# Local attention units taken in pairs on four 64x64 tiles, PSUM as one tile, and a new order of the work

## The chip, the cores and the metric

The kernel runs on one core of a Trainium2 chip. The metric is the time of one execution on the device in microseconds (us), lower is better. Inputs are prepared on the host before the launch (laid out, padded, sliced), and this is not timed.

## The reference

Eight sequences (B = 8) of S = 576 tokens with 8 heads of 64 go through two kinds of attention, whose sum is mixed by a Fourier transform and then sent through a feed-forward layer:

```
q_d, k_d, v_d = means over groups of 4 tokens           # 144 of 576 positions
out_up    = repeat(softmax(q_d k_d^T / 8) v_d, 4)
out_local = softmax(where(|i - j| < 4, q k^T / 8, -1e9)) v
x  = out_up + out_local                                 # [8, 576, 512]
u  = x + real(fft(fft(x, axis=1), axis=2))
un = (u - mean) / sqrt(var + 1e-6)
out = u + max(un @ w1, 0) @ w2                          # w1 512x2048, w2 2048x512, given in float64
```

## The kernel before

The work falls into two stages. The first handles attention and the Fourier mix, sequence by sequence. The second is the feed-forward layer over 36 tiles of 128 tokens, in nine blocks of four tiles.

**Local units.** The band |i - j| < 4 is covered by windows of 64 tokens that start 57 apart. A `Unit` (line 525) holds two windows of one sequence, all 8 heads, so there are 5 units a sequence and 40 in all. The two windows lie on the two halves of the partitions: rows 0-63 and rows 64-127. For each unit `scores` puts the mask into one PSUM bank with two matmuls (line 559) and adds 16 matmuls of 64x64 (line 566), heads times halves. The tile that lies on rows 0-63 writes partitions 0-63, the other writes 64-127. `maxima` (line 579) is one VectorE reduction, `exps` scales the maxima and takes one ScalarE exponential per head (line 584), `transpose_p` turns the probabilities with four matmuls into another bank, `copy_p` brings them back to SBUF, `values` multiplies by v with 16 matmuls into two banks (line 625; column 65 gives the row sum), and `result` divides: two small additions (line 639), one reciprocal, and two products (line 643; four products of half the rows for the middle unit of a sequence). A matmul of 32-bit floats (not a transpose) stands in the trace as two, so a burst of one unit's scores or values shows as 32 matmuls.

**Pooled attention.** `Pooled` (line 416) does two heads at a time on 72 partitions: scores into two banks, two maxima (line 443), four exponentials, eight transposes into two banks, two copies (line 475), values (line 483) and a division. Each of its two heads has a bank, and an instruction never spans two.

**Fourier mix.** `Mix` (line 675) folds the sequence into sums and differences on VectorE and GpSimd, splits each 32-bit operand into a high and a low part, multiplies by sine and cosine matrices (lines 744 and 789), and stores to DRAM. `sequence` gives four outputs of 290 columns, each evacuated by one ScalarE copy (line 751) and one VectorE subtraction (line 754). `store_local` writes the local attention's result of a sequence to DRAM in ten transfers at one place in the order.

**Feed-forward layer.** For each of 16 slices f of the hidden layer `Block.first` has 12 matmuls of 128x512 (line 958), `high` and `low` evacuate (lines 962, 966), `second` has 12 more (lines 976 to 978). Blocks 0 and 1 take f = 0 to 4 first, then f = 5 to 15, and then come the other seven blocks. Each weight quarter (`Quarter`, four per f) is fetched by SyncE and decoded from float64 by ScalarE, GpSimd (line 342), VectorE (lines 350, 353, 356), ScalarE and GpSimd (line 371). `CHUNKS` says which f have their place in SBUF from the start (f < 3); the others get places when earlier pools are closed, the next ones at `close_a`, which frees the local units' tiles.

**PSUM.** Eight banks. `bank()` (line 395) hands them out in turn, from two pools; at `close_a` four of them go to the accumulators of the feed-forward layer and four stay in turn.

**Order.** Every step is an event, and the events are issued in the order of the numbers in `TURNS` (a name's numbers go to its calls one after the other), so each engine's queue and each DMA queue is in program order as that table has it. An instruction that waits holds back all that stand behind it on its engine. Loads and stores stand in SyncE's queue, the accumulating loads (`vsum` and the feed-forward layer's `ut`) in GpSimd's.

Of the kernel before, what the change touches and what calls it, by code (L numbers as in the profile page):

```python
# [17 lines left out]
NUM_V, NUM_QKT, NUM_P = 3, 6, 2  # L18
NUM_PT = 2

KEPT = 290
# [6 lines left out]
        3, 7, 11, 26, 46, 82, 84, 101, 156, 213, 246, 262, 231, 263, 351, 378, 401, 448, 494, 526, 562, 586,  # L28
        622, 665, 729, 748, 826, 898, 883, 900, 993, 1048,
    ),  # L30
    "Pooled.scores": (
        18, 19, 35, 39, 81, 110, 124, 175, 222, 224, 283, 321, 382, 383, 466, 468, 547, 569, 598, 628, 706, 722,
        786, 809, 873, 906, 905, 927, 1014, 1036, 1060, 1130,
    ),
    "Pooled.maxima": (
        21, 23, 48, 66, 89, 117, 137, 188, 228, 244, 300, 327, 390, 413, 482, 512, 574, 578, 609, 641, 715, 736,
        804, 839, 878, 911, 928, 960, 1021, 1044, 1076, 1134,
    ),
    "Pooled.exps": (
        25, 30, 50, 71, 95, 128, 161, 194, 236, 275, 308, 332, 395, 427, 492, 518, 582, 596, 619, 648, 726, 764,  # L40
        813, 843, 885, 920, 954, 987, 1028, 1055, 1090, 1136,
    ),
    "Pooled.transpose_p": (
        28, 37, 56, 80, 107, 144, 173, 199, 252, 286, 328, 345, 418, 435, 497, 531, 588, 600, 627, 672, 740,
        783, 829, 848, 907, 924, 972, 994, 1034, 1067, 1131, 1139,
    ),
    "Pooled.copy_p": (
        32, 53, 69, 86, 127, 160, 177, 209, 277, 307, 331, 366, 426, 461, 502, 534, 595, 617, 645, 685, 761,
        790, 832, 850, 919, 955, 989, 998, 1053, 1093, 1135, 1145,
    ),  # L50
    "Pooled.values": (
        41, 55, 77, 91, 143, 174, 181, 214, 285, 319, 340, 380, 430, 464, 521, 544, 599, 624, 668, 703, 782,
        808, 845, 858, 925, 969, 995, 1003, 1069, 1114, 1138, 1147,
    ),
    "Pooled.result": (
        63, 64, 88, 97, 165, 187, 189, 226, 318, 326, 372, 388, 446, 486, 536, 554, 634, 635, 678, 710, 805,
        825, 866, 867, 959, 975, 1007, 1019, 1108, 1133, 1155, 1158,
    ),
    "Pooled.store": (105, 291, 403, 565, 728, 942, 1096, 1188),
    "Pooled.pack": (103, 233, 399, 561, 727, 882, 1031, 1164),  # L60
    "Mix.half_sum": (
        118, 112, 133, 266, 270, 268, 408, 438, 442, 577, 630, 638, 730, 737, 769, 895, 931, 910, 1059, 1043,
        1079, 1166, 1205, 1191,
    ),
    "Mix.half_difference": (
        121, 99, 142, 260, 248, 302, 421, 449, 452, 585, 613, 614, 744, 750, 774, 912, 913, 914, 1049, 1050,
        1083, 1172, 1177, 1196,
    ),
    "Mix.channels": (
# [4 lines left out]
    ),  # L74
    "Mix.fold": (
# [4 lines left out]
    ),  # L80
    "Mix.split_high": (
# [79 lines left out]
    ),  # L161
    "constants": (83,),
    "clear_yz": (93,),
    "close_b": (1193,),
    "close_a": (1226,),
    "close_e": (1304,),
    "close_d": (1401,),
# [1034 lines left out]
```

## Time and profile before

| | |
|---|---|
| median of 3 runs | 1155.38 us (1148.1 to 1157.35) |
| the profiled execution | 1145.82 us, span 1144.0 us |
| busy: TensorE / VectorE / ScalarE / GpSimd | 1108.0 / 545.4 / 358.4 / 293.5 us |
| mean granted clock of TensorE | 0.99 |
| moved by DMA | 123.07 MB |

Names in the profile: PE is TensorE, PEld its weight loads, DVE VectorE, ACT ScalarE, POOL GpSimd, SP SyncE. A busy time is counted once where instructions overlap. "L566" is line 566 of the kernel. In a timeline or chain "x32" means 32 instructions taken together. The chain is the sequence of instructions and waits that ended last, followed back from the end.

### The profile page before, as it was taken

The numbers are of one execution on the slowest core, as the hardware profiler recorded it, in microseconds if no ns is written. First come the engines' busy times: TensorE is split into PE (matmuls) and PEld (weight loads), VectorE is DVE, ScalarE is ACT, GpSimd is POOL, SyncE is SP. The second block draws the span as 40 slices with busy tenths as digits, with TensorE's granted clock in tenths as the row PEclk, the third lists the DMA queues.
The fourth block names the chain that finished last, engine by engine and source line by source line (L and its number), as shares of the span: only waits on it lengthen the run. The fifth ranks groups of instructions, "written<-read, shape, count | busy, mean of one in ns | idle before, by whom it ended". The sixth has DMA issues, their size and how long they took to land.

```text
span 1144.0 us, 20389 instructions
## 1 busy us (share of the span) xinstructions
PE 1108.0 (97%) x8172; PEld 935.8 (82%) x8172; DVE 545.4 (48%) x1226; ACT 358.4 (31%) x1050; POOL 293.5 (26%) x411
## 2 busy tenths in 40 slices
PE   7899999899889999999999999999999999999998
PEld 6788888889778788888888888888888888888886
DVE  4889999899878776322212222222222222222111
ACT  4777767767544443111111111111111111111110
POOL 2444545355574553203002002001101100200000
PEclk7999999999999999999999999999999999999999
DMA  8888777777685332506006005105103302400000
GB/s 257 269 257 252 215 240 247 234 217 181 181 188 161 109 123 93 110 1 148 1 1 147 1 1 129 19 1 121 27 1 95 53 1 71 77 1 37 1 1 37
DMA packets 57901, 123.07 MB, mean 108 GB/s; under 512 B 7280, under 2 KB 7408, under 8 KB 57552
## 3 DMA queue, kind: packets, MB, share of 16 engines
q1 hardware_dynamic: 44288, 92.23, 24.6%
q0 software_dynamic: 13520, 29.55, 14.7%
q8 instruction: 64, 1.05, 0.4%
q14 instruction: 29, 0.24, 0.1%
HBM read 89.88 MB, written 30.74 MB: 105 GB/s over the span
## 4 chain that ended last, share of the span: by engine, by line
PE 79%; DVE 10%; DMA 6%; issue 2%; SPq 1%; ACT 1%; POOL 0%; DVEq 0%; ACTq 0%; POOLq 0%
PE hps L958 34%; PE acc L976 11%; PE acc L978 11%; PE acc L977 11%; DMA vsum<-in_vg_dram 3%; PE y L744 2%; PE av L625 1%; PE avd L483 1%; PE sc L566 1%; PE tpn L932 1%; DVE sums L552 1%; DMA raw<-in_wq_dram 1%; PE mix L789 1%; DVE xeo L710 1%; DVE w L697 1%
## 5 line engine op out<-in xcount | busy, mean ns | idle before, releaser
L966 DVE SCALAR_TENSOR_TENSOR hl<-hps,hh 128x512 fp32r<-128x512 f32 x144 | 99.1, 690 | 456.3 <-ACT hh L962 456.3
L958 PE MATMUL hps<-unT,w1h 128*128 128x512 f32 x1152 | 309.9, 392 | 0.0
L962 ACT ACTIVATE hh<-hps 128x512 fp32r<-128x512 f32 x144 | 86.0, 598 | 539.2 <-PE hps L958 533.9
L958 PEld LDWEIGHTS hps<-unT,w1h 128*128 128x128 f32 x1152 | 215.5, 188 | 45.7
L976 PE MATMUL acc<-w2h,hh 128*128 128x512 f32 x576 | 227.3, 395 | 0.2 <-ACT hh L962 0.2
L978 PE MATMUL acc<-w2h,hl 128*128 128x512 f32 x576 | 225.5, 392 | 0.0
L977 PE MATMUL acc<-w2l,hh 128*128 128x512 f32 x576 | 225.4, 391 | 0.0
L958 PE MATMUL hps<-unT,w1l 128*128 128x512 f32 x576 | 155.2, 392 | 0.0
L978 PEld LDWEIGHTS acc<-w2h,hl 128*128 128x128 f32 x576 | 108.3, 188 | 24.0 <-DVE hl L966 0.4
L958 PEld LDWEIGHTS hps<-unT,w1l 128*128 128x128 f32 x576 | 108.3, 188 | 23.6
L976 PEld LDWEIGHTS acc<-w2h,hh 128*128 128x128 f32 x576 | 108.3, 188 | 23.4 <-ACT hh L962 0.6
L977 PEld LDWEIGHTS acc<-w2l,hh 128*128 128x128 f32 x576 | 108.3, 188 | 22.4
L917 POOL TENSOR_TENSOR rstd<-rstd,mhalf 128x1 f32<-128x1 f32 x36 | 19.9, 554 | 300.3 <-DVE rstd L916 299.1
L902 POOL DMA_DIRECT2D ut<-ux x40 | 35.5, 1002 | 206.7 <-DMA ut<-um 206.3
L584 ACT ACTIVATE sb<-sc,mx 128x64 f32<-128x64 f32 x320 | 69.8, 329 | 2.0 <-PE tpl L596 0.8
L941 DVE TENSOR_TENSOR unT<-tpn,unT 128x512 fp32r<-128x512 f32 x36 | 24.8, 688 | 55.4 <-ACT unT L938 55.4
L552 DVE TENSOR_REDUCE sums<-qkT 128x224 f32<-128x896 f32 (+4 forms) x48 | 44.4, 945 | 11.0 <-DMA qkT<-in_qk_dram 9.2
L566 PEld LDWEIGHTS sc<-qkT 64*64 64x64 f32 x1280 | 46.1, 141 | 3.8 <-DMA qkT<-in_qk_dram 0.6
L625 PE MATMUL av<-vaug,pT 64*64 64x65 f32 x1280 | 47.4, 224 | 1.3 <-DMA vaug<-in_vw_dram 0.7
L724 POOL TENSOR_TENSOR fl<-xeo,fh 128x512 fp32r<-128x512 f32 x32 | 42.0, 1334 | 21.8 <-ACT fh L721 16.3
L625 PEld LDWEIGHTS av<-vaug,pT 64*64 64x64 f32 x1280 | 42.2, 138 | 6.3 <-issue 2.9
L566 PE MATMUL sc<-qkT 64*64 64x64 f32 x1280 | 46.4, 225 | 0.1
(97 smaller groups left out, 1368.1 us busy)
## 6 DMA issues: line engine op xcount, KB each, us to landing
qkT<-in_qk_dram SPq DMA_DIRECT2D x40, 512.0 KB
raw<-in_wq_dram SPq DMA_DIRECT2D x64, 256.0 KB
vaug<-in_vw_dram SPq DMA_DIRECT2D x40, 260.0 KB
out_dram<-ut SPq DMA_DIRECT2D x36, 256.0 KB
um<-o SPq DMA_DIRECT2D x16, 512.0 KB
ut<-ux POOLq DMA_DIRECT2D x32, 256.0 KB, 5.1
ut<-ud POOLq DMA_DIRECT2D x32, 256.0 KB, 5.4
vsum<-in_vg_dram POOLq DMA_DIRECT2D x24, 292.5 KB, 6.7
```

Source lines behind the costliest of these rows:

```text
L552: nc.vector.tensor_reduce(out=to, in_=x[:, :, a - g0 : e - g0], axis=AX.X, op=ALU.add)
L566: nc.tensor.matmul(sc[r, a * W : (a + 1) * W], self.qkT[r, 0, a // 2, o : o + W], self.qkT[r, 1, a // 2, o : o + W], start=False, stop=Tru ...
L584: nc.scalar.activation(out=self.sb[:, a], in_=self.sc[:, a * W : (a + 1) * W], func=AF.Exp, scale=0.125, bias=self.mx[:, a : a + 1],)
L625: nc.tensor.matmul(av[r, a, :], pT[r, 4 * hh + a], va[r, 4 * hh + a, :], start=True, stop=True)
L724: nc.gpsimd.tensor_sub(out=self.fl[:, t], in0=self.x[t], in1=self.fh[:, t].bitcast(F32))
L902: nc.gpsimd.dma_start(out=to, in_=ux[b][k0 : k0 + m, :], accum_op=ALU.add)
L958: nc.tensor.matmul(hps, a[:, c, :], unT[:, x, c, :], start=(i == 0), stop=(i == len(mms) - 1))
L962: nc.scalar.activation(out=hh, in_=self.hps[f], func=AF.Relu)
L966: nc.vector.scalar_tensor_tensor(out=hl, in0=self.hps[f], scalar=0.0, in1=self.hh[f].bitcast(F32), op0=ALU.max, op1=ALU.subtract)
L976: nc.tensor.matmul(acc, hh, w2h, start=start, stop=False)
L977: nc.tensor.matmul(acc, hh, w2l, start=False, stop=False)
L978: nc.tensor.matmul(acc, hl, w2h, start=False, stop=stop)
```

## The change

Units are paired. `Duo` takes the next two units in the order `ORDERS` and does their `scores`, `maxima` and `values` together; the loads, exponentials, transposes, copies and divisions stay with each unit. One unit of a pair is crossed: its matmuls on rows 0-63 write partitions 64-127 and those on rows 64-127 write partitions 0-63, so that two units' matmuls, issued in turn, name four different 64x64 tiles. The host swaps the two windows of such a unit's v to match. All eight banks become one tile; `Banks.take(n)` gives n neighbouring free banks, the ones free for longest, and `done` gives them back at the place of the last reader. So these become one instruction over two banks: the pair's maxima, the pooled maxima and copy, a unit's division, and the evacuation of two `sequence` outputs. The accumulators of the feed-forward layer take banks in the same way. `NUM_P` goes from 2 to 4 (buffers of probabilities), one pooled buffer of two heads replaces two, `CHUNKS` starts with 2 in place of 3, `store_local` becomes two events of five transfers, and all numbers of `TURNS` are new.

```diff
-NUM_V, NUM_QKT, NUM_P = 3, 6, 2
-NUM_PT = 2
+NUM_V, NUM_QKT, NUM_P = 3, 6, 4
+NUM_PT = 1
...
-CHUNKS = (3, 5, 9, 16)
+CHUNKS = (2, 5, 9, 16)
...
+    def take(self, n=1):
+        runs = [range(i, i + n) for i in range(0, len(self.held), n)]
+        runs = [r for r in runs if not any(self.held[b] for b in r)]
+        run = min(runs, key=lambda r: (max(self.since[b] for b in r), r[0]))
...
-            for hl, sp in enumerate(self.sps[h0]):
-                nc.vector.tensor_reduce(
-                    out=mx[:, 2 * hl : 2 * hl + 2], in_=sp, axis=AX.X, op=ALU.max, negate=True
-                )
+            nc.vector.tensor_reduce(
+                out=mx.rearrange("g (h t) -> g h t", h=2), in_=self.sp[h0], axis=AX.X, op=ALU.max, negate=True
+            )
...
+        def rows(self, n, out=False):
+            n ^= out and self.cross
+            return slice(n * W, (n + 1) * W)
...
+    class Duo:
...
+        def scores(self):
+
+            sc = self.sc = bank(self, "sc", n=2)
...
+            for a in range(H):
+                for x in self.pair:
+                    o = x.wins[a % 2][0] - x.s0
+                    for n in range(2):
+                        r = x.rows(n)
+                        nc.tensor.matmul(
+                            x.sc[x.rows(n, True), a * W : (a + 1) * W],
...
+        def maxima(self):
+            mx = p2.tile([P, 2, H], F32, name="mx", bufs=2)
+            scores = self.sc.rearrange("p x (h w) -> p x h w", h=H)
+            nc.vector.tensor_reduce(out=mx, in_=scores, axis=AX.X, op=ALU.max, negate=True)
+            nc.scalar.mul(out=mx, in_=mx, mul=0.125)
...
+        def values(self):
+            for x in self.pair:
+                x.av = bank(x, "av", n=2)[:, :, : 4 * (D + 1)].rearrange("p b (h d) -> p b h d", h=4)
+            for h in range(H):
+                for x in self.pair:
+                    for n in range(2):
...
+            nc.vector.tensor_sub(out=yl, in0=self.y[i], in1=yh.bitcast(F32))
+            done((self, i), "y")
...
-        def store_local(self):
+        def store_local(self, back):
...
-                self.accs = [pacc[0].tile([P, DM], F32, name="acc") for _ in range(TILES)]
+                self.accs = [bank((self, t), "acc")[:, 0] for t in range(TILES)]
...
+ORDERS = [(0, 1, 2, 3, 4), (1, 0, 2, 4, 3)]
```

## Rows read from the trace of the kernel before

**Rows 1.** The profile's page: busy time of the engines with their share of the span, and the granted clock of TensorE in 40 slices.

```profile
PE 1108.0 (97%) x8172; PEld 935.8 (82%) x8172; DVE 545.4 (48%) x1226; ACT 358.4 (31%) x1050; POOL 293.5 (26%) x411
...
PEclk7999999999999999999999999999999999999999
```

**Rows 2.** Busy time by stretch. Columns: from and to, length, then for PE, PEld, DVE, ACT and POOL the busy us with the number of instructions, the granted clock, the mean busy share of the 16 DMA engines, GB/s.

```profile
0.00:25.00 25.00, 18.14 (x213) 15.68 (x214) 9.85 (x20) 8.63 (x32) 5.62 (x16) 0.66 0.86 264
25.00:300.00 275.00, 257.83 (x4148) 233.97 (x4146) 250.03 (x650) 198.96 (x714) 134.50 (x173) 0.99 0.79 232
300.00:329.30 29.30, 21.79 (x193) 19.72 (x192) 21.18 (x53) 11.19 (x26) 20.17 (x25) 0.94 0.65 159
329.30:455.00 125.70, 125.52 (x574) 103.09 (x572) 99.66 (x211) 51.87 (x128) 63.84 (x108) 1.00 0.44 130
455.00:1144.00 689.00, 684.68 (x3053) 563.37 (x3051) 164.68 (x297) 87.75 (x150) 69.34 (x90) 1.00 0.21 46
```

**Rows 3.** The same columns for two stretches of 100 us inside the second of those.

```profile
25.00:125.00 100.00, 91.87 (x1566) 82.99 (x1564) 88.58 (x234) 73.19 (x272) 46.54 (x59) 1.00 0.85 254
100.00:200.00 100.00, 95.77 (x1449) 86.71 (x1447) 94.65 (x243) 72.20 (x254) 49.12 (x63) 1.00 0.77 236
```

**Rows 4.** The chain that ended last: its shares from 25 to 300 us by line, and a stretch of it on PE (start, us until the next piece, what).

```profile
by line: PE y L744 6.8%; PE av L625 6.0%; PE avd L483 5.8%; PE sc L566 5.4%; DMA vsum<-in_vg_dram 4.9%; DVE sums L552 4.9%; issue 4.7%; DVE xeo L710 3.7%; DVE w L697 3.6%; DMA raw<-in_wq_dram 3.0%; DVE mxd L443 2.9%; DVE mx L579 2.8%; SPq L
...
93.58 1.25 PE avd L483 x16
94.83 0.34 PE sc L559 x2
95.17 0.93 PE sc L566 x32
96.10 0.64 PE sp L438 x8
```

**Rows 5.** Pieces of the same chain on DVE, near 120 and near 162 us. L643 has 256 elements a partition, L697 255, L807 512.

```profile
119.05 0.76 DVE xb L643 x2
...
161.42 0.66 DVE w L697 x2
162.08 0.61 DVE o L807
```

**Rows 6.** The timeline: one unit's values (start, us, engine, line, instructions).

```profile
153.85 1.01 PEld L625 LDWEIGHTS av<-vaug,pT 64*64 64x64 f32 x32 [0.16 <-issue]
153.85 1.15 PE L625 MATMUL av<-vaug,pT 64*64 64x65 f32 x32
```

**Rows 7.** Groups of instructions from 25 to 300 us: line, engine, operation, names, shapes, count | busy us, mean ns of one | idle time before them and what ended it.

```profile
L584 ACT ACTIVATE sb<-sc,mx 128x64 f32<-128x64 f32 x304 | 66.3, 329 | 2.0 <-PE tpl L596 0.8
L625 PE MATMUL av<-vaug,pT 64*64 64x65 f32 x1184 | 43.1, 222 | 1.3 <-DMA vaug<-in_vw_dram 0.7 <-issue 0.3 <-DVE odt L498 0.2
L566 PE MATMUL sc<-qkT 64*64 64x64 f32 x1184 | 40.6, 218 | 0.0
...
L579 DVE TENSOR_REDUCE mx<-sc 128x8 f32<-128x512 f32 x38 | 25.6, 680 | 0.1
L443 DVE TENSOR_REDUCE mxd<-sp 72x2 f32<-72x288 f32 x60 | 24.2, 444 | 2.9 <-PE sp L438 2.7
...
L643 DVE TENSOR_TENSOR xa<-av,rs 128x256 f32<-128x256 f32 (+1 forms) x46 | 18.0, 418 | 1.2
L643 DVE TENSOR_TENSOR xb<-av,rs 128x256 f32<-128x256 f32 (+1 forms) x44 | 17.4, 421 | 0.8
...
L559 PE MATMUL sc<-maskb,identb 64*64 64x512 bf16 x74 | 14.7, 392 | 4.2 <-ACT sb L584 2.4 <-ACT pT L614 0.8 <-DVE xa L643 0.5
L754 DVE TENSOR_TENSOR yl<-y,yh 128x290 fp32r<-128x290 f32 x24 | 10.3, 451 | 0.5 <-ACT yh L751 0.4
L639 DVE TENSOR_SCALAR rs<-av 128x4 f32<-128x4 f32 x74 | 9.0, 152 | 5.6 <-PE av L625 5.4
L356 DVE SCALAR_TENSOR_TENSOR wt<-raw,wt 128x256 int32<-128x256 int32 x12 | 6.0, 504 | 0.4
L342 POOL TENSOR_SCALAR wt<-wt 128x256 f32<-128x256 f32 x12 | 5.2, 431 | 12.2 <-ACT wt L337 11.5 <-ACT mxd L449 0.7
L353 DVE SCALAR_TENSOR_TENSOR wt<-raw,wt 128x256 int32<-128x256 int32 x12 | 5.1, 425 | 0.4
L371 POOL TENSOR_TENSOR w2l<-wt,w2h 128x256 fp32r<-128x256 f32 x6 | 4.6, 771 | 9.2 <-ACT w2h L367 8.5 <-DVE xeo L710 0.6
L350 DVE TENSOR_SCALAR wt<-wt 128x256 int32<-128x256 int32 x12 | 3.4, 283 | 0.0
```

**Rows 8.** The chain from 300 to 330 us.

```profile
300.90 7.45 DMA ux<-xa
...
313.73 5.12 DMA ut<-um
...
319.37 0.85 POOL ut L902
...
321.67 7.81 PE y L744 x46
```

**Rows 9.** The first 25 us: the first unit's scores and the first pooled scores in the timeline.

```profile
8.96 1.97 PE L566 MATMUL sc<-qkT 64*64 64x64 f32 x32
...
15.38 2.20 PE L438 MATMUL sp<-sums 64*72 64x144 f32 x16 [2.31 <-DVE sums L552]
```

More of the change, by code (lines that the diff above doesn't have):

```diff
@@ L239, with __init__, give @@
 WARM_UP = 40
+class Banks:
+    def __init__(self, tile, width, count=8):
+        self.tile, self.width = tile, width
+        self.held, self.since, self.turn = [False] * count, list(range(-count, 0)), 0
+    def take(self, n=1):
+        runs = [range(i, i + n) for i in range(0, len(self.held), n)]
+        runs = [r for r in runs if not any(self.held[b] for b in r)]
+        run = min(runs, key=lambda r: (max(self.since[b] for b in r), r[0]))
+        for b in run:
+            self.held[b] = True
+        return run
+    def give(self, run):
+        for b in run:
+            self.held[b], self.since[b] = False, self.turn
 TINY_HIGH = 1.125 * 2.0**-15
@@ L387, with bank, done @@
     nc.gpsimd.memset(odt[:, :, DM:], 0.0)
-    pbank = ExitStack()
-    banks = [ctx.enter_context(tc.tile_pool(name="banks", bufs=8 - TILES, space=PSUM))]
-    banks.append(pbank.enter_context(tc.tile_pool(name="more_banks", bufs=TILES, space=PSUM)))
-    first_bank = banks[:1]
-    pools = {}
-    def bank(name, rows=P):
-        banks.append(banks.pop(0))
-        return banks[-1].tile([P, DM], F32, name=name, tag="ps")[:rows]
+    psum = ctx.enter_context(tc.tile_pool(name="psum", bufs=1, space=PSUM))
+    banks = Banks(psum.tile([P, 8, DM], F32, name="banks"), DM)
+    pools, runs = {}, {}
+    def bank(owner, name, rows=P, n=1):
+        run = runs[owner, name] = banks.take(n)
+        return banks.tile[:rows, run[0] : run[0] + n]
+    def done(owner, name):
+        banks.give(runs.pop((owner, name)))
     xa, xb = (px.tile([P, NSL, DM], F32, name=f"x{j}") for j in "ab")
@@ L616, in copy_p @@
                     nc.scalar.copy(out=pT[r], in_=tpv[r])
-        def values(self):
-            pT, va = self.pT, self.va
-            self.av = [bank("av")[:, : 4 * (D + 1)].rearrange("p (h d) -> p h d", h=4) for _ in range(2)]
-            for hh, av in enumerate(self.av):
-                for a in range(4):
-                    for n2 in range(2):
-                        r = slice(n2 * W, (n2 + 1) * W)
-                        nc.tensor.matmul(
-                            av[r, a, :], pT[r, 4 * hh + a], va[r, 4 * hh + a, :], start=True, stop=True
-                        )
+            done(self, "tpl")
         def result(self):
@@ L796, in even_out @@
             nc.scalar.copy(out=self.even[t], in_=ps)
+            done((self, t, 0), "mix")
         def unfold(self, t, minus):
@@ L812, in unfold @@
             )
+            if len(self.mixed.setdefault(t, [])) == 1:
+                done((self, t, 1), "mix")
+            self.mixed[t].append(minus)
         def store_mixed(self):
@@ L867, in plan @@
                 at(self.store_ends)
-            at(self.store_local)
+            for back in range(2):
+                at(self.store_local, back)
     NU = B * NPAIR
@@ L873 @@
     units = [Unit(u) for u in range(NU)]
+    turns = [NPAIR * b + m for b in range(B) for m in ORDERS[b % 2]]
+    duos = [Duo(n, [units[u] for u in turns[2 * n : 2 * n + 2]]) for n in range(NU // 2)]
     quarters = [Quarter(n) for n in range(4 * NF)]
@@ L1008 @@
         mixes[b].plan()
-    for u in units:
-        u.plan()
+    for x in (*units, *duos):
+        x.plan()
     at(constants)
@@ L1065 @@
     warm = raws[0][:, : P // 2].bitcast(BF16)
-    for _ in range(WARM_UP):
-        nc.tensor.matmul(bank("warm")[:, :P], warm, warm, start=True, stop=True)
+    for i in range(WARM_UP):
+        nc.tensor.matmul(banks.tile[:, i % 8, :P], warm, warm, start=True, stop=True)
     with tc.manual_schedule():
```

386 lines of the change are left out of this document (192 added, 194 removed), and 64 rows, old and new, of the table TURNS.

## The prediction

> **What bounds the kernel now.** I read the page first: PE is busy 97% of the span at a clock near full [rows 1]. That share averages over stages, so the second view was busy time by stretch [rows 2]. From 329.3 us on, the feed-forward layer, PE is busy 810 of 815 us while DVE falls from 79% to 24%. The change leaves these matmuls as they are, so nothing is to be had there. What can move is the time until the layer starts: a head of 25 us, a body of 275 us and a junction of 29.3 us. In the body PE is busy 257.8 us (93.7%), DVE 250.0 us (90.9%) and the DMA engines 79%; ACT (72%) and POOL (49%) have room. So two engines bound the body almost equally. The third view, the chain of waits, says the same: no line has more than 7% of it, and PE and DVE pieces take turns [rows 4]. A gain on one engine alone would stop at the other; the change takes work from both.
>
> **PE's part.** A burst of 32 matmuls of a unit's scores takes 0.93 us, of 16 pooled values of about the same shape on 72 rows 1.25 us [rows 4]: 29 against 78 ns for one. So two tiles that lie on different halves of rows and columns already run beside each other, 58 ns for each two. Pooled scores, eight matmuls of 144 columns in 0.64 us [rows 4], are less than half as dear by column, and their tiles lie on different halves of the rows but on the same columns; so sharing columns does not stop it. Sharing rows, the other thing that four tiles need, is in no row. If four run as two do now, two units' bursts cost what one costs now. The body has 37 units (1184 matmuls by 32) [rows 7]; each costs 0.34 us of mask, 0.93 us of scores [rows 4] and about the same for values: 2.2 us. Half of 37 x 2.2 is 41 us. The other end is 0: the tiles wait for each other. I take 41, since the cheap cases in the trace are those with different tiles. PE would be busy 217 us of the body, and stop being its bound.
>
> The Trainium skill speaks against this in "TensorE: Matmul & The Clock Gate", section "The mechanism" of Part 3: a weight load overlaps matmuls in flight only when their row groups differ, and here two tiles always share one. In this trace 32 weight loads, 1.01 us, lie inside 1.15 us of the matmuls on the same rows [rows 6], so the rule as it is worded does not hold for a tile's own next load; for two tiles on the same rows no run shows it yet. By the rule the saving on PE would be near 0, which is the first rival below.
>
> **DVE's part.** In the body the change removes 19 of 38 L579, 30 of 60 L443, 37 of 74 L639, 45 of 90 L643 and 12 of 24 L754 [rows 7]: 143 instructions. Their elements stay, so each saves only a fixed part. L579 has 512 elements in 680 ns and L754 290 in 451 ns [rows 7], about 1.03 ns an element, which leaves 0.15 us fixed. In a full queue part of that overlaps: two of half the size take 0.66 to 0.76 us, one whole 0.61 [rows 5], so 0.05 to 0.15 is saved. That makes 7 to 21 us; I take 0.08 each, 11 us, since DVE's queue is mostly full. Four of the twelve weight quarters decoded in the body also leave it (`CHUNKS` 3 to 2), at 14.5 / 12 = 1.2 us of DVE each [rows 7]: 4.8 us. DVE is left with 234 us (224 to 238).
>
> **The body's new length.** DVE is now the largest. The busiest engine reaches 93.7% now, DVE alone 90.9%, and in its best 100 us 94.7% [rows 2, 3]. 234 / 0.937 is 250 us, 25 less than now. The ends are 224 / 0.947 = 237 and 238 / 0.909 = 262. ACT loses work too and stays near three quarters; its cover is DVE's. DMA moves the same bytes but for 1 MB of 64: 0.79 x 275 = 217 us of all 16 engines, less 1.6%, which at the 85% of the first 100 us [rows 3] needs 251 us. So DMA is just covered by DVE, and no more.
>
> **The moved quarters.** The four quarters (f = 2) now wait for `close_a` and fall into the junction, where the chain runs through a DMA of the mix, POOL's accumulating load and its fold, and the last `y` matmuls [rows 8]. On POOL they cost 4 x (0.43 + 0.77) = 4.8 us, on DVE 4.8 us, and POOL is already busy 20.2 of 29.3 us there [rows 2, 7]. If all stand ahead of the fold, 4.8 us; if they stand behind, 0, because f = 2 is first used two slices after the layer starts, and DVE has 26 us free up to 455 us [rows 2]. I take 2.5. The two halves of `store_local` let one half's transfers leave SP earlier; the present chain waits 7.45 us at those stores [rows 8]. How SP then stands is open, and I count 0 with 3 us to either side.
>
> **The head.** The first pair needs two units' q and k, so the first scores come later than 9 us; but the pooled scores, which need all five units, come at 15.4 us [rows 9] and hold the order up anyway. 0 to 3 us; I take 1. **PSUM:** in the feed-forward layer the accumulators draw on all eight banks; PE is 99% busy there, so 0.
>
> **Sum.** -25 + 2.5 + 1 = -21.5 us. The profiled execution was 1145.8 us, 1144.0 of it span; on it the sum gives 1124. The median of the three runs shown is 1155.4, 9.6 above, and I assume that this level stays: **1134 us**. The ends of the terms give 1155.4 - 38 = 1117 and 1155.4 - 13 + 4.8 + 3 = 1150.
>
> **Rivals.** *Four tiles do not run together.* Rows shared by two tiles make them take turns, PE keeps 257.8 us, and at 93.7 to 95.8% [rows 2, 3] the body is 269 to 275 us. With 3.5 us for junction and head: 1153 to 1159, say 1155. For it speaks that no row shows two tiles on one half of the rows; against it the pooled scores on shared columns.
>
> *DMA holds the body.* If the share stays at 79%, since SP's queue is in order and loads stand behind waiting stores, the body is 214 / 0.79 = 270 us, and the time 1154. Against it: 85% over the first 100 us.
>
> *Slower: a pair's banks come free too late.* The place is PE's queue ahead of `Duo.scores` and `Duo.values`. Two banks are held until both units' exponentials are done, 8 x 0.218 = 1.74 us longer than for one unit [rows 7], and values need four of eight banks at once, behind two divisions of about 1.1 us (0.76 [rows 5] and the small ones). If all of it showed it would be 3.9 us for each of the 18.5 pairs in the body. PE has 217 us of work and 17 us of idle as now, so 41 us more, 2.2 us for each pair, brings the present length back; at 3 us for each the body is 289 us and the time 1173. For it: the wait for `sb` before L559 is already there, 2.4 us in all [rows 7]; against it: it is small, and the new order has exponentials between.
>
> *Much faster.* Both engines wait less for each other, DVE reaches 97% with 224 us: 231 us, the time 1155.4 - 44 + 1 = 1112.
>
> That the change does not do what it says I exclude: the pair and its crossing are explicit.
>
> **How the numbers follow.** About 1%, 11.6 us, is what a measurement of this kernel can tell from no change: faster is below 1143.8, slower above 1167. Chances: forecast 0.62, no overlap 0.14, DMA 0.07, slower 0.07, much faster 0.08, and 0.02 for what I have not seen. Faster: 0.56 of the forecast (its upper end counts as no change), 0.08, and 0.03 from rivals that hold only in part, 0.67. Slower: 0.07, 0.02 and 0.01 from a no-overlap case with a bad junction, 0.10. The rest is 0.23. The range 1113 to 1153 holds most of the forecast and of the much faster case and half of the two rivals without gain: about 0.8. The forecast's own range is 1117 to 1150.
>
> **What would show it.** Four tiles: 64 matmuls of a pair's scores in about 1 us, not 1.9. DVE: one maxima of 1024 elements near 1.2 us, and DVE the busiest engine of the body, with PE below 90% there. The first feed-forward matmul should start near 308 us, not 329. Wrong would be: bursts of a pair as long as two of now; PE waiting long ahead of L559's successor for exponentials or divisions; DMA above 90% while all engines idle; a pause of PE at f = 2.

## The result and the profile after: no gain, 0.7% slower

The changed kernel takes 1161.11 us (median of 14 runs, 1153.74 to 1164.96); the kernel before, on the same chip, 1152.72 us (14 runs, 1147.02 to 1159.7). The ratio is 1.0067 (95% interval 1.0039 to 1.0095). The forecast was 1134 us. The profiled execution took 1158.67 us, 12.9 more than that of before, 1145.82 us, which is faster than any of the 14 above: of the difference between the two profiles some 4 us belong to that one execution.

From the page of the changed kernel, busy times and granted clock, against [rows 1]:

```profile
PE 1091.3 (94%) x8172; PEld 918.2 (79%) x8172; DVE 549.9 (48%) x1070; ACT 348.7 (30%) x982; POOL 298.1 (26%) x411
...
PEclk7768999998989999999999999999999999999999
```

DVE has 156 instructions fewer and is busy 4.5 us longer. Of the first twelve slices of the clock (29 us each) only the first was below 9 before; now the first four, the tenth and the twelfth are.

Busy time by stretch, columns as in [rows 2], up to the first feed-forward matmul: the kernel before (329.3 us) ...

```profile
0.00:125.00 125.00, 110.01 (x1776) 98.67 (x1777) 98.43 (x253) 81.83 (x304) 52.16 (x75) 0.93 0.86 256
125.00:329.30 204.30, 187.74 (x2775) 170.70 (x2775) 182.62 (x468) 136.95 (x468) 108.13 (x139) 0.98 0.74 210
```

... and the changed kernel (337.15 us):

```profile
0.00:125.00 125.00, 93.98 (x1509) 83.23 (x1509) 82.12 (x162) 68.86 (x243) 44.89 (x67) 0.75 0.76 225
125.00:337.15 212.15, 185.33 (x3019) 166.07 (x3018) 192.41 (x395) 137.57 (x456) 112.67 (x141) 0.94 0.77 217
```

Read the fifth column, DVE. Ahead of the layer it works 98.43 + 182.62 = 281.05 us before and 274.53 after: 6.5 less. It idles 48.25 us before and 62.62 after: 14.4 more. Together +7.9 us, the delay of the layer's start. All of the idle time is new in the first 125 us (26.6 to 42.9); behind them DVE is busy 89.4% before and 90.7% after. By 125 us the changed kernel has done 16 us less of DVE's work, and carries that on. The other 4.7 us are lost in the layer, right behind its start: PE is busy 1.8 us longer there, since the last outputs of the mix stand behind the layer's first matmuls, and idles 2.9 us more. Matmul 240 of the layer comes at 392.0 us before and at 406.1 after; from there to the end the changed kernel is 1.7 us faster.

The prediction's own body, 25 to 300 us, in the changed kernel:

```profile
25.00:300.00 275.00, 237.20 (x4065) 211.51 (x4058) 230.66 (x468) 180.77 (x625) 124.76 (x155) 0.89 0.77 221
```

DVE is busy 83.9% of it and PE 86.3%; neither is near 93.7%. The prediction had DVE as the busiest engine of the body; here it is that only behind 125 us (90.7% against 87.4%).

**The four tiles.** The timeline of PE. One unit's scores before:

```profile
26.02 1.09 PE L566 MATMUL sc<-qkT 64*64 64x64 f32 x32
```

A pair's values, mask and scores after:

```profile
38.03 1.92 PE L648 MATMUL banks<-qkT 64*64 64x64 f32 x64
...
48.03 1.16 PE L672 MATMUL banks<-vaug,pT 64*64 64x65 f32 x62 [0.30 <-ACT pT L595]
...
50.30 0.41 PE L642 MATMUL banks<-maskb,identb 64*64 64x512 bf16 x4
50.54 1.10 PE L648 MATMUL banks<-qkT 64*64 64x64 f32 x64
```

64 matmuls of two units take 1.10 us where one unit's 32 took 1.09 at the same clock. The first row is the same burst at the lower of the clock's two levels, 1.2 GHz: 1.92 us.

**VectorE's operations.** Groups of DVE ahead of the layer's first matmul. Before:

```profile
L579 DVE TENSOR_REDUCE mx<-sc 128x8 f32<-128x512 f32 x40 | 27.0, 680 | 0.1
L686 DVE TENSOR_TENSOR xs<-xa,xb 128x512 f32<-128x512 f32 x24 | 18.6, 775 | 0.1
L697 DVE TENSOR_TENSOR w<-xm 128x255 f32<-128x255 f32 x24 | 9.6, 415 | 0.1
L353 DVE SCALAR_TENSOR_TENSOR wt<-raw,wt 128x256 int32<-128x256 int32 x14 | 6.0, 425 | 0.5
```

After:

```profile
L660 DVE TENSOR_REDUCE mx<-banks 128x16 f32<-128x1024 f32 x20 | 24.3, 1215 | 6.0 <-PE banks L648 5.9
L714 DVE TENSOR_TENSOR xs<-xa,xb 128x512 f32<-128x512 f32 x24 | 19.7, 826 | 0.6 <-DMA xa<-odt 0.4
L725 DVE TENSOR_TENSOR w<-xm 128x255 f32<-128x255 f32 x24 | 12.5, 521 | 1.4 <-POOL xm L717 1.4
L355 DVE SCALAR_TENSOR_TENSOR wt<-raw,wt 128x256 int32<-128x256 int32 x13 | 9.0, 690 | 0.4
```

The merged reduction saves 2.7 us, 0.13 for each of the 20 that went; 0.05 to 0.15 was forecast. But operations that the change does not touch cost more each: 415 to 521 ns, 775 to 826, 425 to 690. The timelines of DVE and of POOL at one place show why:

```profile
316.40 0.55 DVE L963 TENSOR_SCALAR un<-ut,mv,rstd 128x512 f32<-128x512 f32 x1 [0.44 <-POOL rstd L956]
...
317.19 0.42 DVE L725 TENSOR_TENSOR w<-xm 128x255 f32<-128x255 f32 x1
...
319.07 1.49 DVE L963 TENSOR_SCALAR un<-ut,mv,rstd 128x512 f32<-128x512 f32 x1
320.48 0.41 DVE L725 TENSOR_TENSOR w<-xs 128x255 f32<-128x255 f32 x1
320.82 1.48 DVE L725 TENSOR_TENSOR w<-xm 128x255 f32<-128x255 f32 x1
322.22 1.42 DVE L785 TENSOR_TENSOR yl<-banks,yh 128x580 fp32r<-128x580 f32 x2
```

```profile
318.76 1.52 POOL L717 TENSOR_TENSOR xm<-xa,xb 128x512 f32<-128x512 f32 x1
320.53 1.49 POOL L752 TENSOR_TENSOR fl<-xeo,fh 128x512 fp32r<-128x512 f32 x1 [0.25 <-POOL xm L717]
```

Two DVE operations of 0.55 and 0.42 us take 1.49 and 1.48 where they start behind a POOL operation that reads two SBUF operands, and they end some 0.3 us after it has ended (320.28 and 322.02), which looks more like standing than like running slowly. PE waits at this place for `yl`, which stands behind them in DVE's queue, 5.13 us where the kernel before waited 0.64; some 2.0 us of that are the two operations' extra time, the rest is other work of DVE in the queue.

```profile
303.06 0.38 PE L789 MATMUL mix<-chanm,yl 128*128 128x256 f32 x1 [0.64 <-DVE yl L754]
...
323.02 0.58 PE L820 MATMUL banks<-chanm,yl 128*128 128x256 f32 x1 [5.13 <-DVE yl L785]
```

**The head.** PE's long pauses of the first 62 us, in its timeline after:

```profile
31.77 2.10 PE L484 MATMUL banks<-vsum,ptd 72*72 72x65 f32 x16 [4.67 <-DMA vsum<-in_vg_dram]
...
60.65 1.64 PE L672 MATMUL banks<-vaug,pT 64*64 64x65 f32 x49 [5.33 <-DMA vaug<-in_vw_dram]
```

The kernel before waits 1.22 us for `vsum` at the same place, where its first unit's values and one more unit's scores stand ahead of it. Right behind both pauses the granted clock is at its lower level; over the first 125 us its mean is 0.75 (0.93 before).

### The profile page after: what moved, and what is told of

Read it like the earlier page. It is cut to its first block, busy times and chain, and to the rows that moved or that the text cites. A ratio compares the mean times of both kernels' runs of the same rounds, so it can differ in the third digit from the quotient of the medians.

```text
span 1156.5 us, 20097 instructions
## 1 busy us (share of the span) xinstructions
PE 1091.3 (94%) x8172; PEld 918.2 (79%) x8172; DVE 549.9 (48%) x1070; ACT 348.7 (30%) x982; POOL 298.1 (26%) x411
## 4 chain that ended last, share of the span: by engine, by line
PE 80%; DVE 10%; DMA 5%; issue 2%; ACT 1%; POOL 1%; SPq 0%; DVEq 0%; POOLq 0%
PE banks L998 33%; PE banks L1017 11%; PE banks L1019 11%; PE banks L1018 11%; PE banks L774 3%; DMA vsum<-in_vg_dram 2%; PE banks L484 2%; DMA vaug<-in_vw_dram 1%; PE banks L672 1%; PE banks L971 1%; PE banks L820 1%; PE banks L577 1%; DVE wt L355 1%; PE banks L466 1%; DVE xb L612 1%
## 5 line engine op out<-in xcount | busy, mean ns | idle before, releaser
L998 PE MATMUL banks<-unT,w1h 128*128 128x512 f32 x1152 | 309.6, 392 | 1.2 <-DVE unT L980 1.2
L998 PEld LDWEIGHTS banks<-unT,w1h 128*128 128x128 f32 x1152 | 215.2, 188 | 47.0 <-DVE unT L980 1.6
L1017 PE MATMUL banks<-w2h,hh 128*128 128x512 f32 x576 | 226.6, 393 | 2.3 <-DVE hl L1006 2.3
L1019 PE MATMUL banks<-w2h,hl 128*128 128x512 f32 x576 | 225.0, 391 | 0.0
L1018 PE MATMUL banks<-w2l,hh 128*128 128x512 f32 x576 | 224.7, 390 | 0.0
L998 PE MATMUL banks<-unT,w1l 128*128 128x512 f32 x576 | 154.9, 391 | 0.0
L1017 PEld LDWEIGHTS banks<-w2h,hh 128*128 128x128 f32 x576 | 108.2, 188 | 25.1 <-DVE hl L1006 2.7
L998 PEld LDWEIGHTS banks<-unT,w1l 128*128 128x128 f32 x576 | 108.1, 188 | 23.5
L1019 PEld LDWEIGHTS banks<-w2h,hl 128*128 128x128 f32 x576 | 108.2, 188 | 23.3
L1018 PEld LDWEIGHTS banks<-w2l,hh 128*128 128x128 f32 x576 | 108.2, 188 | 22.4
L555 DVE TENSOR_REDUCE sums<-qkT 128x224 f32<-128x896 f32 (+4 forms) x48 | 43.7, 943 | 10.7 <-DMA qkT<-in_qk_dram 10.6
```

The source lines that it names most:

```text
L555: nc.vector.tensor_reduce(out=to, in_=x[:, :, a - g0 : e - g0], axis=AX.X, op=ALU.add)
L998: nc.tensor.matmul(hps, a[:, c, :], unT[:, x, c, :], start=(i == 0), stop=(i == len(mms) - 1))
L1017: nc.tensor.matmul(acc, hh, w2h, start=start, stop=False)
L1018: nc.tensor.matmul(acc, hh, w2l, start=False, stop=False)
L1019: nc.tensor.matmul(acc, hl, w2h, start=False, stop=stop)
```

## The experiments

Each ratio is to the kernel before, runs of the same chip; the changed kernel has 1.0067 (1.0039 to 1.0095). The runs come from several chips, so ratios are compared, and a difference of two ratios is sure only to about half a per cent, 5 to 7 us.

**Is PE still a bound?** Two runs give PE more work: units that are not crossed, and discarded matmuls ahead of each pair's mask.

```diff
 def crossed(b, m):
-    return ORDERS[b % 2].index(m) % 2 ^ b % 2
+    return 0
```

> Edit: the changed kernel with no unit crossed, so that both units of a pair use the same two tiles, and a pair's bursts of scores and values take 1.8 us again instead of 0.9; order, banks and merged instructions stay. Theory V: PE is not what bounds the body, so the 37 to 41 us of PE work that come back cost little, 1158 to 1168 us, and the granted clock rises since PE is busier. Rival P (PE still bounds the body): 20 us or more, above 1178 us. Rival C: the clock comes back to above 0.98 and the time falls to 1155 us or below.

1170.41 us, 1.012 (1.0066 to 1.0174). A pair's burst now takes nearly twice as long (timeline, at the higher level of the clock, then the two stretches):

```profile
140.38 2.03 PE L648 MATMUL banks<-qkT 64*64 64x64 f32 x64
```

```profile
0.00:125.00 125.00, 95.87 (x1481) 85.35 (x1482) 80.31 (x159) 65.74 (x233) 44.27 (x65) 0.86 0.77 224
125.00:347.60 222.60, 204.12 (x3048) 186.19 (x3047) 194.28 (x397) 140.28 (x466) 112.15 (x143) 0.98 0.75 207
```

So crossing does what it says; but the 20 pairs x 2 bursts x 0.93 us = 37 us that it is worth at the higher clock cost only 6 us of time by the ratios (10 us at the layer's start in the profiles). PE's busy time ahead of the layer rises by 20.7 us, not 37, since the granted clock is higher. Most of what the four tiles save is not on the path. The time lies between the two expectations, nearer to theory V.

```diff
+FILL = 9
...
+            for _ in range(FILL):
+                cols = maskb.unsqueeze(1).to_broadcast([P, H, W])
+                nc.tensor.matmul(sc[:, 0].rearrange("p (h w) -> p h w", h=H), identb, cols, start=True, stop=True)
             for x in self.pair:
```

> Edit: the changed kernel with nine matmuls of 128x512 (bf16) ahead of each pair's mask, into a bank that the mask overwrites: about 39 us of PE work at 2.4 GHz more, nothing else changed. Rival C: the clock stays up (mean above 0.98) and the time falls by 5 us or more in spite of the added work. Theory V: the waits stay where they are; the clock rises somewhat, and the time stays within 5 us or grows by up to 15 us.

1178.88 us, 1.0203 (1.0146 to 1.026), slightly more than theory V allowed. The clock's means rise to 0.86 up to 125 us and 0.96 behind, and do not pay for the added work.

**Is it the clock?** Discarded matmuls on a free bank ahead of four of PE's waits:

```diff
...
+    for place, n in ((42.9, 20), (119.9, 24), (234.9, 6), (1103.9, 20)):
+        events.append((False, place, -1, partial(warm, n)))
```

> What it tells apart: order and waits are left alone; ahead of four of TensorE's waits stand matmuls on a free PSUM bank (20, 24, 6 and 20 of 128 x 512 bf16, discarded), which occupy part of the time in which it would stand. Theory C (the pauses cost above all by the clock that falls after them): the time at 1.2 GHz before the FFN falls from 89 to under 40 us, the last pooled score of the third sequence comes at 108 us or earlier (116), and the time falls by 6 to 12 us. Rival (what counts is what TensorE waits for; a faster clock behind the waits only makes the next one longer): the time changes by 3 us or less, whatever the clock.

1161.55 us, 1.0092 (1.0063 to 1.0122): nothing gained. The clock's mean rose to 0.88 in the first 125 us, and the third sequence's last pooled score came 4 us earlier (112). The lead was gone again by the layer (341.5 us), with a new wait of PE ahead of it, 6.7 us for GpSimd's part of the decoding (L344). Two things limit this run: the first filling itself held PE until 35.7 us, where the pooled values had started at 31.8, and behind the head the clock's mean was 0.91, so that by the means some 70 us at 1.2 GHz are left (89). So the clock is not acquitted.

**Is it a buffer, or the order of the head?** Seven runs change a buffer or move work in the first sequences.

```diff
-NUM_V, NUM_QKT, NUM_P = 3, 6, 4
+NUM_V, NUM_QKT, NUM_P = 4, 6, 4
...
-            self.sb = p2.tile([P, H, W], F32, name="sb", bufs=NUM_P)
+            self.sb = p2.tile([P, H, W], F32, name="sb", bufs=NUM_P - 1)
```

> Edit: the changed kernel with four buffers for a unit's v in place of three, and three in place of four for the probabilities before the transpose, which makes the room. Theory V (a pair needs two v tiles at once, so with three buffers the second load of the next pair waits for the present pair's values, and all that stands behind it in SyncE's queue waits too): SyncE's empty stretch from 27 to 42 us goes, the 7.1 us that PE's values wait for v fall under 2 us, the values of the first three sequences end within 8 us of the kernel before instead of 15 to 23 us later, and the time falls from 1161 to 1143 to 1150 us. Rival C (TensorE's clock, 1.2 GHz in some 71 us of the stretch from 25 to 337 us, is the cause by itself): clock and time stay, 1157 to 1163 us. Rival O (the new order of the work is at fault as a whole): under 4 us gained.

1159.54 us, 1.0056 (1.0013 to 1.0099). A fourth v buffer, paid for with one of `sb`, gains nothing that can be told. No run gives back the second pooled buffer (`NUM_PT` was 2).

```diff
-        0, 4, 63, 37, 98, 204, 101, 208, ...
+        0, 4, 63, 37, 98, 204, 97.6, 208, ...
```

> What it tells apart: only the v load of unit 6 is moved, on SyncE's queue, ahead of the packing of sequence 0's pooled rows, behind which it landed at 60.6 us and TensorE stood 5.3 us. Theory H in two parts (the early wait for the pooled values made the first half of the lag, this load the second): the 5.3 us pause goes, the third sequence's last pooled score comes 4 to 8 us earlier (108 to 112 us), the time falls by 3 to 6 us. Rival (the pause is taken over by the next wait): under 2 us.

1158.93 us, 1.0059 (1.0025 to 1.0093). The 5.3 us pause goes, others take its place, and the third sequence is at 116 us as in the changed kernel.

```diff
 "Unit.transpose_p"[1]: 44 -> 33.5     "Unit.copy_p"[1]: 46 -> 34      "Duo.values"[0]: 58 -> 34.2
 "Unit.result"[0, 1]: 65, 64 -> 34.4, 34.3     "Pooled.scores"[3]: 32 -> 34.6
 "Pooled.transpose_p"[1]: 33 -> 34.8   "Unit.exps"[3]: 57 -> 53.9      "Unit.load_v"[6]: 101 -> 97.6
```

> What it tells apart: in the changed kernel TensorE's order of work in the head has the pooled values of sequence 0 (which wait for the summed v until 31.6 us) ahead of the first pair's values, which run at 40 us only; SyncE's queue then stands until 41.7 us at the v load that needs the buffer they free. Here the transposes, the values and the results of the first pair are put ahead of that wait, and the v load of unit 6 ahead of the packing of the pooled rows. Theory H (the lag of about 20 us is made by this order): the third sequence's last pooled score falls from 116 to 100 us or less, the first FFN matmul from 337 to 327 us or less, and the time lies 8 us or more under the changed kernel's, at 0.980 to 0.995 of the kernel before. Rival B (TensorE's slow clock and VectorE's work hold the body, the order of the head does not): the first FFN matmul stays within 4 us of 337 and the ratio at 1.002 to 1.009.

1159.78 us, 1.0072 (1.0042 to 1.0101); with four v buffers as well 1160.38, 1.0085 (1.0052 to 1.0118). The third sequence comes 3 us earlier, the layer does not. Then the order of sequence 0 set anew, twice (79 numbers of `TURNS` in the first, 86 in the second):

> What it tells apart: nothing is left out; the order of sequence 0 in the changed kernel is set anew (the five qk loads first on SyncE's queue, the first pair's maxima ahead of the later sums on VectorE, exps, transposes and values of the first two pairs as early as their data allow, the pooled values behind them, the packing ahead of the first weight quarter). Theory H (a lag of about 20 us is made in the first three sequences, by an order in which VectorE idles while pairs wait for loads, for each other and for the pooled values, and is carried to the FFN): VectorE's busy time in the first 125 us rises from 82 to 90 us or more, the first FFN matmul comes at 328 us or earlier (337), and the time falls by 8 us or more, at or under the kernel before's. Rival B (behind the head VectorE sets the pace and the lag is taken back or made anew whatever the head does): first FFN matmul at 334 us or later, time within 4 us of the changed kernel's.

1165.14 us, 1.0105 (1.006 to 1.015). The layer starts at 335.2 us, and DVE's busy time in the first 125 us is 83.94, not 90. One wait took the place of another, in DVE's timeline:

```profile
36.08 0.16 DVE L502 TENSOR_SCALAR rsd<-banks 72x4 f32<-72x4 f32 x1 [10.28 <-PE banks L491]
```

> What it tells apart: nothing is left out; the first new head put the transposes and values of the pooled rows, which wait for the summed v until 33.8 us, ahead of the scores of the third pair, the values of the second and the sums of the next sequence, and VectorE stood 10.3 us behind them. Here those come first. Theory H: the third sequence's last pooled score comes at 104 us or earlier (116 in the changed kernel, 112 with the first new head, 96 before), the first FFN matmul at 330 us or earlier (337), and the time falls 6 us or more under the changed kernel's. Rival T (a lead at sequence 2 is lost again by the FFN, since in the stretch behind it the order's waits hold whatever came before): the third sequence is earlier as said, and the first FFN matmul still at 334 us or later, the time within 4 us of the changed kernel's.

1168.33 us, 1.0155 (1.0077 to 1.0232); neither theory, it is worse from the start (118 us at the third sequence, 345.8 at the layer). The last run takes the pairs out of the first ten units and gives these two sequences the order of the kernel before:

```diff
     class Unit:
+        def scores(self): ...
+        def maxima(self): ...
+        def values(self): ...
     class Duo:
-            for fn in (self.scores, self.maxima, self.values):
+            for fn in (self.scores, self.maxima, self.values) if self.n >= 5 else ():
```

> What it tells apart: nothing is left out; the changed kernel with its first ten units (sequences 0 and 1) scored, reduced and multiplied one by one, as in the kernel before, and with that kernel's order for these two sequences (a few PSUM releases drawn forward so that the banks suffice); from sequence 2 on the pairs and their order. Theory H (the pairs themselves make the lag in the head: two loads before the first scores, one reduction for two units, two units' values behind one another): VectorE's busy time in the first 125 us rises from 82 us to 92 or more (98 before), the first FFN matmul comes at 329 us or earlier (337), the time falls to 1142 to 1153 us, at or under the kernel before's. Rival O (the lag is not of the pairing but of the memory and the banks that the change gave out otherwise, or arises anew where the pairs begin): VectorE's busy time there rises by less than 5 us or the first FFN matmul stays at 334 us or later, and the time at 1157 us or over.

1180.43 us, 1.0263 (1.0234 to 1.0291), the layer at 361.2 us: theory H's numbers are missed by far. But the graft made waits of its own, so it does not acquit the pairs either. One of them in PE's timeline, and the first 125 us:

```profile
57.77 2.00 PE L679 MATMUL banks<-vaug,pT 64*64 64x65 f32 x32 [7.66 <-DMA vaug<-in_vw_dram]
```

```profile
0.00:125.00 125.00, 90.75 (x1406) 79.05 (x1408) 72.12 (x145) 61.89 (x224) 38.52 (x57) 0.81 0.72 210
```

**Is it the weights' decoding?** Without the four quarters of f = 2 (slice 2 uses the weights of slice 1):

```diff
+            if self.f == 2:
+                return
...
-            w1h, w1l = wts[f, 1]
+            w1h, w1l = wts[1 if f == 2 else f, 1]
```

> Edit: the changed kernel without fetch and decode of the four weight quarters of f = 2; the feed-forward layer takes f = 1's weights in their place, so the amount of matmul work is the same. This is a part of the computation left out. Theory F (the quarters moved behind close_a hold up the start of the feed-forward layer on DVE): the first feed-forward matmul comes 2 to 5 us earlier than 337 us, PE's pauses from 337 to 375 us (5 us) go, and the time falls by 5 to 9 us. Rival: other work of DVE and GpSimd holds the start, and the time falls by less than 2 us.

1157.74 us, 1.0033 (0.9997 to 1.0068). That is 0.34% less than the changed kernel, between the two expectations, and it cannot be told from no gain: the intervals overlap. In the profile DVE's work ahead of the layer falls by 4.9 us (to 269.6), and the layer starts no earlier (337.4 us). Then VectorE's joins of the first eight quarters on one column, in the changed kernel and in the kernel before:

```diff
-            t = self.t
+            t, hi, lo = ((x[:, :1] if self.n < 8 else x) for x in (self.t, self.hi, self.lo))
```

> What it tells apart: the changed kernel with the three joining operations of the first eight weight quarters done on one column only (the values of those weights are left unjoined, so that part of the computation is left out); this takes some 12 us of VectorE's work out of the 337 us ahead of the FFN and nothing from TensorE. Theory D (VectorE sets the pace of the stretch before the FFN in the changed kernel): time falls by 7 to 12 us, first FFN matmul at 326 to 331 us. Rival (order and waits in chains across engines): falls by 0 to 4 us.

> What it tells apart: the same edit in the kernel before (the first eight weight quarters unjoined, so that part of the computation is left out): 11 us less on VectorE, nothing less on TensorE. If VectorE is no less a bound there than in the changed kernel, it gains as much as that one (7 to 12 us); if TensorE is the bound of the kernel before, as the prediction had it, it gains 0 to 4 us.

1160.98 us, 1.0065 (1.0041 to 1.0089), and 1147.42 us, 0.9949 (0.9926 to 0.9972). Theory D fails: nothing in the changed kernel, 6 us in the one before, where the gain lies between the two that were expected. In the changed kernel DVE was busy only 4 us less ahead of the layer (81.90 + 188.44), and idled 6 more. That would fit if nothing waits soon for a join, so that it fills DVE's gaps. The 6 us before are not explained: in its profile the layer starts at 329.7 us, no earlier, but the profile it is compared with is of an execution faster than the median.

**Is it GpSimd?** Its three subtractions in the mixing write zeros, in the changed kernel and before, and then twice over:

```diff
-            nc.gpsimd.tensor_sub(out=halves[1][:, t, :DM], in0=xa[:, t], in1=xb[:, t])
+            nc.gpsimd.memset(halves[1][:, t, :DM], 0.0)
...
```

> What it tells apart: in the changed kernel GpSimd's three subtractions of the mixing (half difference, minus fold, low split) write zeros instead of reading two operands (so the odd half and the low parts of the mixing are left out). Theory S (VectorE's operations on SBUF alone take about twice as long beside a GpSimd operation that reads two operands, and this ate most of what the merged operations saved): operations of lines 352, 714, 725 and 738 show their short durations throughout (about 280, 680, 415 and 420 ns), VectorE's busy time ahead of the FFN falls by 12 to 18 us (274 in the changed kernel). Theory D on top: the time falls by 8 us or more. Rival: VectorE's durations stay as they are, or fall without the first FFN matmul coming over 4 us earlier.

> What it tells apart: the kernel before with GpSimd's three subtractions of the mixing writing zeros (the odd half and the low parts of the mixing are left out), as was done to the changed kernel, which it made 15 us faster. If the changed kernel suffers more from GpSimd (theory S: VectorE's excess beside it was 8 us before and 18 after), the kernel before gains 3 to 8 us, and the two come to within 5 us of each other. If GpSimd's work weighs on both alike, it gains 12 us or more and the gap of some 8 us between them stays.

> What it tells apart: as the run with GpSimd's zeros in the changed kernel (the odd half and the low parts of the mixing are left out), with every zero written twice, so that GpSimd's own time (107 us in its three subtractions ahead of the FFN, 51 us as zeros) is back at about 103 us while it still reads nothing. Theory S (what counts is that VectorE's operations on SBUF are slowed beside a GpSimd operation that reads two operands): VectorE's durations stay short and the time stays within 4 us of the single zeros (1141 to 1149 us). Theory G (what counts is GpSimd's own time, in the chains of the mixing and in its queue): the time rises back by 8 us or more, to 1153 us or over.

Changed, zeros: 1144.96 us, 0.9924 (0.9898 to 0.9951), 16 us less. Before, zeros: 1150.49 us, 0.9985 (0.9949 to 1.002), no difference that can be told, and less than either expectation. Changed, zeros twice: 1147.26 us, 0.9958 (0.9925 to 0.999), 12 us less than the changed kernel. The groups of DVE with zeros, lines as above:

```profile
L714 DVE TENSOR_TENSOR xs<-xa,xb 128x512 f32<-128x512 f32 x24 | 16.3, 682 | 1.3 <-POOL xeo L739 1.2
L741 DVE TENSOR_TENSOR xeo<-w 128x256 f32<-128x256 f32 x32 | 13.1, 416 | 0.4
L725 DVE TENSOR_TENSOR w<-xm 128x255 f32<-128x255 f32 x24 | 10.5, 436 | 0.0
```

The stretches with zeros once, and with zeros twice:

```profile
0.00:125.00 125.00, 90.23 (x1608) 78.84 (x1609) 84.39 (x177) 71.76 (x254) 31.26 (x70) 0.85 0.81 233
125.00:324.20 199.20, 177.91 (x2920) 160.06 (x2919) 173.81 (x380) 133.38 (x444) 61.82 (x137) 0.94 0.79 226
```

```profile
0.00:125.00 125.00, 95.57 (x1630) 84.43 (x1632) 87.25 (x182) 73.47 (x260) 43.42 (x96) 0.82 0.81 238
125.00:319.70 194.70, 178.20 (x2900) 160.78 (x2897) 173.08 (x375) 131.92 (x440) 91.14 (x202) 0.91 0.81 229
```

With zeros DVE needs 258.2 us ahead of the layer, 16.3 less, and the layer starts 13 us earlier. Twice the zeros put POOL back to 134.6 us of its 157.6, and most of the gain stays: it is the reading beside DVE that costs, not POOL's own time. Zeros also wait for no operands, so what stands behind GpSimd's results could come earlier; but in the changed kernel the waits of PE, DVE and ACT that GpSimd's three subtractions end come to some 4 us ahead of the layer, too few for 13. In the kernel before DVE's work falls by 7.7 us with zeros, and DVE idles 10.6 us more instead; that PE holds it there is likely (303 of 332 us busy), not shown. Without GpSimd's reads the changed kernel would be level with the kernel before or a little faster: 0.9924 / 0.9985 = 0.994, and 0.997 with zeros twice, which cannot be told from 1.

Last, one subtraction moved to VectorE with nothing left out: the half difference, or the minus fold.

```diff
-            nc.gpsimd.tensor_sub(out=halves[1][:, t, :DM], in0=xa[:, t], in1=xb[:, t])
+            nc.vector.tensor_sub(out=halves[1][:, t, :DM], in0=xa[:, t], in1=xb[:, t])
```

```diff
-            eng, op = (nc.gpsimd, ALU.subtract) if minus else (nc.vector, ALU.add)
+            eng, op = (nc.vector, ALU.subtract) if minus else (nc.vector, ALU.add)
```

> What it tells apart: nothing is left out; in the changed kernel the half difference is worked out by VectorE in place of GpSimd: some 24 operations of 0.68 us (16 us) more on VectorE ahead of the FFN, 35 us less on GpSimd, and VectorE's excess beside it falls by a third (6 us). Theory G: the time falls by 4 to 10 us. Theory D (VectorE's work sets the pace): it rises by 5 to 12 us. If neither holds, within 3 us.

> What it tells apart: nothing is left out; in the changed kernel the minus fold is worked out by VectorE in place of GpSimd: 32 operations of 0.42 us (13 us) more on VectorE ahead of the FFN, 28 us less on GpSimd, right between the channels and the high split, so that the mixing's chain is shorter by one step from engine to engine. Theory G: the time falls by 4 to 10 us. Theory D: it rises by 4 to 10 us.

1169.7 us, 1.0172 (1.0124 to 1.022), and 1166.66 us, 1.0154 (1.0109 to 1.0198). The second stretches:

```profile
125.00:349.00 224.00, 194.40 (x3063) 173.39 (x3061) 202.36 (x420) 141.99 (x471) 95.09 (x127) 0.92 0.74 210
```

```profile
125.00:345.60 220.60, 191.05 (x3050) 171.96 (x3050) 198.92 (x422) 140.53 (x466) 95.67 (x119) 0.92 0.74 211
```

By the ratios the two rise by 12 and 10 us, about as theory D had it. Where the work of DVE in the mixing grows the kernel gets slower, and where it shrinks it gets faster: behind the first 125 us the stretch is DVE's busy time plus 20 to 25 us in all of these runs (212.15 - 192.41, 199.20 - 173.81, 194.70 - 173.08, 224.00 - 202.36, 220.60 - 198.92). It is not every operation of DVE that counts: the 4 to 5 us that went with the joins or with f = 2 became idle time. None of the runs with nothing left out beats the kernel before.

## Why the prediction was wrong, by its steps

- **PE: the saving right, the clock left out.** Rows show 64 matmuls in 1.10 us; masks, scores and values of all 40 units cost 65.7 us where they cost 110.4, in spite of the lower clock. The forecast took 41 us off 37 units. But PE's busy time ahead of the layer fell only from 297.8 to 279.3 us, mostly since the rest of its work took longer at the lower granted clock (a pooled value 255 ns in place of 230): the forecast priced all of it at the clock of before, without a reason. The Trainium skill's rule ("TensorE: Matmul & The Clock Gate", "The mechanism" of Part 3), by which a weight load overlaps matmuls only when the row groups differ, is not borne out as that sentence words it: two tiles of each row half run together here. (The start of the section also lets a load into the background weight buffer go ahead; no row tells the two apart.) The rival built on it is out.
- **DVE's merged instructions: right, a little low.** The five merged groups ahead of the layer cost some 14 us less; 0.08 for each instruction makes 12 there, 11 in the body.
- **"DVE is left with 234 us", a fall of 16: a term is missing.** The 4.8 us of the moved quarters leave the body, but not the time ahead of the layer (13 quarters are joined there after, 14 before). So some 13 us less were due there, and 6.5 came. The sum took durations from [rows 7] as if they were the operation's own; some hold waiting for GpSimd, and this waiting doubled. With zeros DVE's work ahead of the layer falls by 7.7 us in the kernel before and by 16.3 in the changed one; that is 8.6 us more, and it eats more than half of what the merges saved. A join (L355) took 690 ns in place of 425.
- **"The busiest engine reaches 93.7%", 234 / 0.937 = 250: the step that failed.** It lets DVE's idle time in the body shrink from 25 to 16 us with DVE in PE's place as the busiest engine; the runs show it growing. Ahead of the layer DVE idles 62.6 us, 14.4 more than before. Behind the first 125 us it is busy 90.7% (89.4% before), in the first 125 its share fell from 79% to 66%, and these 16 us are twice the delay of the layer. As I read it, the old share belonged to an order in which two engines mostly had work ready, and not to the engine; why the new order leaves DVE idle early is open.
- **The head, "0 to 3 us": the same step in small, and wrong.** I looked at what the first scores wait for, not at what waits behind the pooled values and behind the v loads in an in-order queue. Six runs that order the head otherwise left DVE's busy time there at 72 to 86 us (98 before). Whether pairing makes that lag, or its order, or the buffers, stays open.
- **The moved quarters, 2.5 us (0 to 4.8): not refuted.** The run without them is 0.34%, 4 us, lower, within the noise, and its layer starts no earlier.
- **Rivals.** DMA did not hold the body (0.77 of its engines there, 0.79 before). A pair's banks were not late: PE's idle time ahead of the mask matmuls is 3.4 us in all ahead of the layer, 7.7 before. Ahead of a pair's values it is 11.5 us (1.3 before), 7.1 of it for loads of v. That the kernel got slower, as this rival had it, came by other means: DVE's waiting for GpSimd grew, and the head idled.

What of the slowdown is shown: taking GpSimd's reads away gives the changed kernel 16 us and the kernel before 2 (interval including 0), so some 14 us of difference between the two hang on them (11 with zeros written twice). What is only accounted for: the idle time of the first 125 us, which no run cured, and what part the clock has in it.

## What to carry to other kernels

Where two engines share a bound, do not divide the new sum of work by the old busy share; ask in each stage what the engine waits for once the other is quicker, and count the head apart. Before work is taken off the engine that shares the bound with VectorE, look at the spread of VectorE's durations by line: where the same operation takes two or three times its shortest time beside GpSimd, that waiting is hidden only as long as another engine is the bound. The merges of instructions saved what they promised here, and the kernel as a whole still got slower; what the pairs cost in freedom of order was not measured apart.

## What the runs showed of the hardware that I had not expected

An operation of VectorE that reads two operands in SBUF can stand until a GpSimd operation that reads SBUF has ended (0.42 us became 1.48 in the rows above); reductions and products that read PSUM keep their time beside it (L660 has 1215 ns with GpSimd's reads and 1217 without). Zeros written by GpSimd leave such operations at their short durations (L714 682 ns, L741 416). The Trainium skill's page "SBUF — State Buffer" says this in "Who interferes with whom": an exclusive lock on a shared pair of ports, against a VectorE instruction with two SBUF inputs only where GpSimd reads. These runs agree, and add that it can be worth 12 to 16 us of 1160. The trace shows one more: L963, with a single large operand in SBUF, stood too (0.55 us became 1.49).

Right behind pauses of PE of 4.67 and 5.33 us the granted clock was at 0.5, and a burst of 64 matmuls behind the first of them took 1.92 us in place of 1.10.
